# A wave-MLP kernel on one core: the first mix matmuls placed later in the order, the last outputs pipelined group by group, x added ahead in DRAM for the first two final steps

## The chip, the cores and the metric

The kernel runs on one core of one Trainium2 chip. The metric is the device time of one execution in microseconds (us). TensorE is PE in the profile, its weight loads PEld, VectorE is DVE, ScalarE is ACT, GpSimd is POOL, SyncE is SP. Times of kernels are medians of 4 to 5 runs (9 for the kernel before). A ratio is the mean time of one kernel's fast runs over that of the kernel before's fast runs of the same rounds, so it is not quite the ratio of the medians that stand beside it.

## The reference, cut to what matters

```python
# x: (8, 4224, 192).  First a causal convolution of 7 taps over the sequence, then:
theta = x @ w_theta
zr, zi = x * np.cos(theta), x * np.sin(theta)
y = einsum('ts,bsd->btd', w_tok_r, zr) + einsum('ts,bsd->btd', w_tok_i, zi)   # 4224 x 4224 each
u = x + y
return u + np.maximum(u @ w_ch, 0.0)
```

Nearly all arithmetic is in the two products with the 4224 x 4224 token matrices, called the *mix* below.

## The kernel before: the parts that matter

The sequence is cut into 33 *chunks* of 128 tokens. A chunk is prepared by: conv (PE) and its copy (ACT); two transposes (PE) and their copies to `uT` (ACT or DVE); two theta products (PE); sines (ACT); two products with x, `product(Z11)` and `product(Z21)`, and four subtractions, `sums` (DVE). They make seven operands, so that seven products do the work of eight.

A *step* is a pair of 128-row blocks of the output, mixed with up to 11 resident chunks (the one block left over makes a step of four runs). It has seven *runs*; each run is one matmul pair per chunk (a *slot*, 128x384 twice). At a run's end the PSUM tile is added into the SBUF tile `pv` by DVE, or copied by ACT: a *give*. There are two PSUM tiles `y`, so a run that opens a new tile waits until an earlier tile has been given. There are 58 steps in three groups of chunks; the last 17 are *final*: they add x, and then make the output (cast on ACT, transpose on PE, copy to `uT` on ACT, channel product on PE, ReLU and add on DVE, DMA out).

DVE also makes the weights of each step: it transposes tiles of the token matrices and forms sums and differences of them, called the *w differences* below.

In the profiles, L404 is the mix, L369 a give by DVE, L196 conv, L138 theta or the channel product, L238 a product with x, L244 the subtractions, L307 a weight transpose, L319 a w difference and L351 the addition of x on POOL. In the changed kernel the lines from L307 on stand one further (L405, L370, L308, L320, L352).

Each engine's order is fixed to the order in which the program emits its instructions. So the emission order in the start loop is an order of queues:

```python
    def between(n):                       # up to n slots of the mix, as far as chunks are ready
        left = more(n)
        if i < 2:
            idle(min(left, 1))            # filler matmuls on zeros
    for i in range(NW + 1):               # NW = 11 chunks; ch = chunk i, old = chunk i - 1
        if ch:  ch.conv(0)
        between(3)
        if old: old.theta(0)
        between(2)
        if ch:  ch.conv(1)
        between(3)
        if old: old.theta(1)
        # ... (loads of chunk i + 3)
        between(2)
        if ch:  ch.transpose(0)
        between(1)
        if ch:  ch.transpose(1)
        between(1)
        if old:
            old.product(Z11); old.product(Z21); old.sums(0); old.sums(1)
            ready[0] = i - 1              # from here the mix may use chunk i - 1
        between(2)
```

```python
    def add_x(self, i):                   # final steps
        if not self.late:                 # late: the last five steps
            xr = wk.tile([P, N], F16, name="xr", tag="xr", bufs=1)
            nc.sync.dma_start(out=xr, in_=xs[rows, :])
            pool(nc.gpsimd.tensor_tensor(out=self.pv[i], in0=self.pv[i], in1=xr, op=ALU.add))
            return
        for cols in (slice(0, HN), slice(HN, N)):      # accumulate in DRAM instead
            pool(nc.gpsimd.dma_start(out=part[...][self.tbs[i], :, cols],
                                     in_=xs[rows, cols], accum_op=ALU.add))
    # ... transposed(): uT = wk.tile([P, 6, P], F16, name="uT", tag="uT")   # two buffers
```

Of the kernel before, what the change touches and what calls it, by code (L numbers as in the profile page):

```python
# [16 lines left out]
def kernel(  # L17
# [42 lines left out]
    NU = (NT + 1) // 2  # L60
    NW = 11
# [5 lines left out]
    NSTEP = start[-1] + NU  # L67
# [13 lines left out]
    def pe(ins):  # L81
        return in_order("pe", ins)
# [7 lines left out]
    def pool(ins):  # L90
        return in_order("pool", ins)
# [68 lines left out]
    Z11, T1, Z21, Z22, T2, T4, T3 = range(7)  # L160

    class Chunk:


        def __init__(self, k, before=None):
            self.k = k
            self.xT = {}
            self.xw = wk.tile([2 * WR, 2, B, D], F16, name="xw", tag="big", bufs=6)
            for a in range(NQ):
                h, lo = a // 2, (a % 2) * WR  # L170
                t0 = token(k, a)
                hist = self.xw[lo : lo + HALO, h, :, :]
                if before is not None:
                    nc.sync.dma_start(
                        out=hist, in_=before.xw[lo + Q : lo + Q + HALO, h, :, :]
                    )
                elif t0 == 0:
                    nc.vector.memset(hist, 0.0)
                else:
                    lo, t0 = lo - HALO, t0 - HALO  # L180
                lo += HALO
                n = (a % 2 + 1) * WR - lo
                nc.gpsimd.dma_start(  # L183
                    out=self.xw[lo : lo + n, h, :, :],
                    in_=x[:, t0 : t0 + n, :].rearrange("b s d -> s b d"),
                )
# [74 lines left out]
    chunks = {}  # L261

    def load_chunk(k):
        if k < NK and k not in chunks:
            chunks[k] = Chunk(k, before=chunks[k - 1] if k % NW else None)

    def active(t):
        return [k for k in range(NK) if start[k] <= t < start[k] + NU]

    def unit(t):  # L270
        return (t + shift) % NU

    class Step:


        def __init__(self, t):
            self.t, self.u, self.ks = t, unit(t), active(t)
            self.n = len(self.ks)
            self.tbs = [tb for tb in (2 * self.u, 2 * self.u + 1) if tb < NT]
            self.pair = len(self.tbs) == 2  # L280
            self.first = t < NU
            self.final = t + NU >= NSTEP
            self.late = self.final and self.n < NW
            self.time = 0.324 * self.n * (7 if self.pair else 4)
            self.st, self.w, self.ub, self.uT, self.pv = {}, {}, {}, {}, []

# [58 lines left out]
        def add_x(self, i):  # L345

            rows = slice(self.tbs[i] * P, (self.tbs[i] + 1) * P)
            if not self.late:
                xr = wk.tile([P, N], F16, name="xr", tag="xr", bufs=1)
                nc.sync.dma_start(out=xr, in_=xs[rows, :])  # L350
                pool(nc.gpsimd.tensor_tensor(  # L351
                    out=self.pv[i], in0=self.pv[i], in1=xr, op=ALU.add  # L352
                ))
                return
            for cols in (slice(0, HN), slice(HN, N)):
                pool(nc.gpsimd.dma_start(
                    out=part[(self.t // NU - 1) % 2][self.tbs[i], :, cols],
                    in_=xs[rows, cols], accum_op=ALU.add,
                ))
# [83 lines left out]
        def outputs(self):  # L443

            found = []
            late = self.late and self.pair
            for i in range(len(self.tbs)):
                at = ((-self.time / 7 + 0.6, 1.2) if late else (0.7, 12.7))[i]
                cast, turn, mix = (1, 2.6, 4.4) if late else (2, 3.6, 5.4)
                for g in range(NG):  # L450
                    d = at + (3 if late else 3.6) * g
                    found.append((at + cast * g, lambda i=i, g=g: self.cast(i, g)))
                    found.append((d + turn, lambda i=i, g=g: self.turn_u(i, g)))
                    found.append((d + mix, lambda i=i, g=g: self.output(i, g)))
            return found

    steps = [Step(t) for t in range(NSTEP)]
# [5 lines left out]
    def step_events(t):  # L463
        found = []
        s = steps[t]
        if t + 1 < NSTEP:
            found += steps[t + 1].w_tasks()
            found.append((1.6, steps[t + 1].load_rows))
            if steps[t + 1].final and not steps[t + 1].late:
                for i in range(len(steps[t + 1].tbs)):  # L470
                    found.append((3.3 + 1.7 * i, lambda i=i: steps[t + 1].add_x(i)))
        if t + 4 < NSTEP and steps[t + 4].late:
            for i in range(len(steps[t + 4].tbs)):
                found.append((3.3 + 1.7 * i, lambda i=i: steps[t + 4].add_x(i)))
        if t + 2 < NSTEP:
            nxt = steps[t + 2]
            for m in (1, 2):
                found.append((1.3 + 3 * (m - 1), lambda m=m: nxt.load_w(m)))
        for at, f in outputs:
            begin = at - sum(s.time for s in steps[:t])  # L480
            if 0 <= begin < steps[t].time:
                found.append((7 * begin / steps[t].time, f))
        if t >= NU - 2:
            new = [k for k in range(NK) if start[k] == t + 2 and k >= NW]
            for k in new:
                found.append((4.5, lambda k=k: load_chunk(k)))
            at = 0.3
            for k in (k for k in range(NK) if start[k] == t + 1 and k >= NW):
                pos = [0, .5, 1.3, 1.6, 2.1, 2.5, 3.1, 3.15, 3.4, 3.6]

                def add(at, j, k):
                    def go():
                        if j == 0:
                            chunks[k].todo = chunks[k].tasks()
                        next(chunks[k].todo)()
                    found.append((at, go))
                for j, p in enumerate(pos):
                    add(at + p, j, k)
                at += 2.6
        return found  # L500


# [27 lines left out]
    def idle(n):  # L530
        for _ in range(n):
            pe(nc.tensor.matmul(
                spare[:, 0, 0:BH], lhsT=noise[:, 0:P], rhs=noise, start=True, stop=True
            ))
# [47 lines left out]
    def stream():  # L582
        for t in range(NSTEP):
            yield from steps[t].mix(step_events(t))

    ready = [-1]
# [3 lines left out]
    def more(n):  # L590

        for i in range(n):
            if need[0] is None:
                need[0] = next(flow, NK)
            if need[0] > ready[0]:
                return n - i
            need[0] = next(flow, NK)
        return 0
# [4 lines left out]
    load_chunk(2)  # L603
    for m in (1, 2):
        steps[1].load_w(m)
    for i in range(NW + 1):
        ch = chunks.get(i) if i < NW else None
        old = chunks[i - 1] if i else None

        def between(n):  # L610
            left = more(n)
            if i < 2:
                idle(min(left, 1))

        if ch:
            ch.conv(0)
        between(3)
        if old:
            old.theta(0)
        between(2)  # L620
        if ch:
            ch.conv(1)
        between(3)
        if old:
            old.theta(1)
        if i == 1:
            for _, f in steps[0].w_tasks():
                f()
        if i + 3 < NW:
            load_chunk(i + 3)  # L630
        between(2)
        if ch:
            ch.transpose(0)
        between(1)
        if ch:
            ch.transpose(1)
        between(1)
        if old:
            old.product(Z11)
            old.product(Z21)  # L640
            old.sums(0)
            old.sums(1)
            ready[0] = i - 1
        between(2)
    nc.vector.memset(wch[:, 1:3, :], 0.0)
    for rows, i, part_w in channel_pieces(moe_w_ch):
# [4 lines left out]
    for at, f in sorted(outputs, key=lambda e: e[0]):  # L651
        if at >= sum(s.time for s in steps):
            f()
# [28 lines left out]
```

## Time and profile before

| | before |
|---|---|
| time, median (3 runs at first, 1479.59 to 1481.64) | 1479.93 us |
| PE busy of the profiled span of 1478.3 us | 1435.8 us |
| PE idle 0 to 120 us | 20.7 us |
| PE idle 1020 to 1040 us | 7.0 us |
| PE idle 1440 us to the end | 12.6 us |

Two lines of the page of the kernel before: busy time by engine, and the engines' shares of the chain that ended last.

```profile
PE 1435.8 (97%) x10086; PEld 904.9 (61%) x10086; DVE 1030.6 (70%) x1050; ACT 361.8 (24%) x461; POOL 435.3 (29%) x655
...
PE 91%; DVE 3%; ACT 2%; DMA 1%; POOL 1%; issue 1%; SPq 0%; DVEq 0%; ACTq 0%; POOLq 0%
```

PE is the bound, so only its idle stretches can be won. The table by windows of the kernel before (window, length, busy us and count of PE, PEld, DVE, ACT, POOL, then granted clock, DMA share, GB/s) shows where they are; nearly all windows left out have PE at 20.00.

```profile
0.00:20.00 20.00, 13.89 (x118) 8.40 (x119) 8.21 (x26) 8.72 (x12) 17.50 (x40) 0.83 1.14 147
20.00:40.00 20.00, 13.29 (x99) 7.80 (x98) 14.46 (x24) 11.17 (x15) 9.73 (x18) 0.74 1.03 155
40.00:60.00 20.00, 16.57 (x150) 10.81 (x149) 15.03 (x24) 17.16 (x24) 11.20 (x20) 0.91 1.22 247
...
100.00:120.00 20.00, 18.72 (x135) 12.06 (x133) 19.15 (x23) 9.12 (x13) 4.29 (x8) 1.00 0.61 144
...
1020.00:1040.00 20.00, 13.04 (x82) 7.88 (x81) 19.57 (x20) 4.45 (x6) 5.40 (x5) 0.92 0.82 216
1440.00:1460.00 20.00, 17.90 (x147) 12.22 (x145) 14.64 (x17) 9.24 (x12) 0.00 (x0) 1.00 0.35 104
1460.00:1480.00 20.00, 7.82 (x74) 6.30 (x71) 5.65 (x6) 6.14 (x8) 0.00 (x0) 0.75 0.36 120
```

The timeline of the kernel before in the start (start us, length us, engine, line, operation, count, and in brackets the idle time before it and what ended it): the first mix matmuls of a chunk wait for its product, and the next chunk's conv (L196) stands behind them.

```profile
23.16 0.80 PE L404 MATMUL y<-z,wt 128*128 128x384 f16 x2 [1.35 <-DVE z L238]
...
24.21 0.85 PE L196 MATMUL pc<-xw,bands 96*64 96x192 f16 x8
...
32.96 1.44 PE L404 MATMUL y<-z,wt 128*128 128x384 f16 x4 [1.51 <-DVE z L238]
...
34.33 0.85 PE L196 MATMUL pc<-xw,bands 96*64 96x192 f16 x8
```

The timeline of the kernel before around 1020 us. Two POOL additions of x (L351) run while DVE has operations with two SBUF inputs (L319, L238), and DVE's pairs take 4.16 and 4.98 us instead of about 1.8. The give (L369) that PE waits for comes late.

```profile
1016.12 3.11 POOL L351 TENSOR_TENSOR pv<-pv,xr 128x1536 f32<-128x1536 f32 x1
1016.76 4.16 DVE L319 TENSOR_TENSOR wt<-wt 128x1408 f16<-128x1408 f16 x2
...
1028.26 4.98 DVE L238 TENSOR_TENSOR z<-z 128x1536 f16<-128x1536 f16 x2
1029.31 3.10 POOL L351 TENSOR_TENSOR pv<-pv,xr 128x1536 f32<-128x1536 f32 x1
1033.28 2.34 DVE L244 TENSOR_TENSOR z<-z 128x768 f16<-128x768 f16 x4
1035.54 0.95 DVE L369 TENSOR_TENSOR pv<-y,pv 128x768 f32<-128x768 f32 x1
...
1036.54 8.66 PE L404 MATMUL y<-z,wt 128*128 128x384 f16 x42 [5.20 <-DVE pv L369]
```

### The profile page before, as it was taken

What the parts mean: (1) busy time and instruction counts of PE and PEld (TensorE: products, weight loads), DVE (VectorE), ACT (ScalarE), POOL (GpSimd) and SP (SyncE); (2) the same over time, 40 slices, a digit from 0 to 9 for tenths busy, and PEclk for the clock granted to TensorE, in tenths of its full rate; (3) what the DMA queues carried; (4) which work ended last, traced back from release to release, by engine and by line L of the source; (5) the groups of instructions that cost most, each with busy time, mean ns of one, the idle gap of its engine ahead of it and who ended that gap; (6) DMA issues with size and microseconds to landing.
All of it is one profiled execution on the core that took longest, in us unless ns stands there. A gap on an engine that the chain in (4) does not pass through costs nothing.

```text
span 1478.3 us, 24435 instructions
## 1 busy us (share of the span) xinstructions
PE 1435.8 (97%) x10086; PEld 904.9 (61%) x10086; DVE 1030.6 (70%) x1050; ACT 361.8 (24%) x461; POOL 435.3 (29%) x655
## 2 busy tenths in 40 slices
PE   6899999999999999999999999998999999999996
PEld 3565666666666666666666666565566666666664
DVE  5894655454558787775766658778889888878675
ACT  4881101111134353000000015254112221212233
POOL 6431211111223322211111133233434343444220
PEclk7999999999999999999999999999999999999998
DMA  9986756564699999977778699999678787999873
GB/s 158 238 170 140 143 102 145 98 148 92 155 220 224 229 201 241 231 179 184 189 174 201 159 199 205 217 221 246 158 183 188 191 176 192 205 229 238 197 196 111
DMA packets 234400, 272.59 MB, mean 184 GB/s; under 512 B 69040, under 2 KB 202544, under 8 KB 234288
## 3 DMA queue, kind: packets, MB, share of 16 engines
q0 software_dynamic: 162464, 92.15, 47.9%
q1 hardware_dynamic: 71824, 178.88, 34.8%
q8 instruction: 79, 1.29, 0.4%
q14 instruction: 33, 0.27, 0.1%
HBM read 245.49 MB, written 108.13 MB: 239 GB/s over the span
## 4 chain that ended last, share of the span: by engine, by line
PE 91%; DVE 3%; ACT 2%; DMA 1%; POOL 1%; issue 1%; SPq 0%; DVEq 0%; ACTq 0%; POOLq 0%
PE y L404 82%; PE v L138 5%; PE tp L153 3%; PE pc L196 2%; DVE z L238 1%; ACT z L233 1%; DVE z L244 1%; POOL st L294 1%; DVE pv L369 1%; POOL xw L183 1%; DMA xw<-in_x_dram 1%; DMA part<-pv 0%; DVE wt L319 0%; DMA xw<-xw 0%; DVE wt L307 0%
## 5 line engine op out<-in xcount | busy, mean ns | idle before, releaser
L404 PE MATMUL y<-z,wt 128*128 128x384 f16 x7656 | 1299.7, 327 | 15.9 <-DVE pv L369 11.8
L404 PEld LDWEIGHTS <-wt 128*128 128x128 f16 x7656 | 738.7, 98 | 485.6 <-issue 23.0
L369 DVE TENSOR_TENSOR pv<-y,pv 128x768 f32<-128x768 f32 x324 | 308.4, 952 | 378.0 <-PE y L404 365.1
L307 DVE STREAM_TRANSPOSE wt<-st 128x1408 f16<-128x1408 f16 (+7 forms) x224 | 326.4, 1462 | 3.9 <-DMA st<-in_moe_w_tok_r_dram 2.1
L294 POOL DMA_DIRECT2D st<-in_moe_w_tok_r_dram x232 | 132.4, 579 | 490.8 <-DVE wt L307 473.4
L294 POOL DMA_DIRECT2D st<-in_moe_w_tok_i_dram x232 | 132.4, 579 | 473.9 <-DVE wt L307 460.4
L319 DVE TENSOR_TENSOR wt<-wt 128x1408 f16<-128x1408 f16 (+7 forms) x216 | 227.2, 1052 | 10.1 <-PE y L404 6.6
L148 ACT ACTIVATE uT<-tp 128x768 f16<-128x768 f16 x127 | 101.6, 811 | 304.6 <-PE tp L153 304.6
L148 ACT ACTIVATE z<-pc 128x768 f16<-128x768 f32 x65 | 52.8, 812 | 386.5 <-PE pc L196 386.5
L367 ACT ACTIVATE pv<-y 128x768 f32<-128x768 f32 x66 | 53.6, 812 | 278.1 <-PE y L404 271.7
L138 PEld LDWEIGHTS <-uT 128*128 128x128 f16 x1056 | 91.9, 99 | 25.3 <-ACT uT L148 5.3
L183 POOL DMA_DIRECT2D xw<-in_x_dram x132 | 76.2, 585 | 37.2 <-DVE wt L307 8.3
L433 DVE SCALAR_TENSOR_TENSOR pv<-v,pv 128x768 f32<-128x768 f32 x66 | 62.3, 948 | 26.9 <-PE v L138 24.1
L244 DVE TENSOR_TENSOR z<-z 128x768 f16<-128x768 f16 x132 | 73.6, 557 | 4.6
L423 ACT ACTIVATE ub<-pv 128x768 f16<-128x768 f32 x66 | 52.6, 836 | 94.5 <-DVE pv L369 76.6
L351 POOL TENSOR_TENSOR pv<-pv,xr 128x1536 f32<-128x1536 f32 x24 | 75.5, 3147 | 0.5 <-DMA xr<-xs 0.3
L233 ACT ACTIVATE z<-v,half_pi 128x768 f16<-128x768 f32 x66 | 59.5, 901 | 40.7 <-PE v L138 40.7
L238 DVE TENSOR_TENSOR z<-z 128x1536 f16<-128x1536 f16 x66 | 63.1, 997 | 3.1 <-ACT z L233 3.1
L138 PE MATMUL v<-wch,uT 128*128 128x192 f16 x528 | 55.2, 250 | 4.4 <-ACT uT L148 4.4
L138 PE MATMUL v<-wth,uT 128*128 128x192 f16 x528 | 55.0, 248 | 3.1 <-ACT z L233 3.1
L233 ACT ACTIVATE z<-v 128x768 f16<-128x768 f32 x66 | 53.1, 804 | 0.0
L153 PE MATMUL tp<-ident,z 128*128 128x128 f16 x396 | 33.8, 223 | 6.7 <-ACT z L233 6.3
(43 smaller groups left out, 193.3 us busy)
## 6 DMA issues: line engine op xcount, KB each, us to landing
part<-pv SPq DMA_DIRECT2D x79, 768.0 KB, 4.1
pv<-part SPq DMA_DIRECT2D x79, 768.0 KB, 5.3
out_dram<-pv SPq DMA_DIRECT2D x66, 384.0 KB, 4.5
st<-in_moe_w_tok_r_dram POOLq DMA_DIRECT2D x136, 176.0 KB, 5.7
st<-in_moe_w_tok_i_dram POOLq DMA_DIRECT2D x136, 176.0 KB, 4.7
xs<-z SPq DMA_DIRECT2D x132, 96.0 KB, 4.0
xw<-in_x_dram POOLq DMA_DIRECT2D x121, 96.0 KB, 6.3
xr<-xs SPq DMA_DIRECT2D x24, 384.0 KB, 3.6
```

Source lines behind the costliest of these rows:

```text
L138: pe(nc.tensor.matmul(v[:, k, b * D : (b + 1) * D], lhsT=tT[:, 3 * k + b + i, :], rhs=w[:, 2 * b + i, :], start=(i == 0), stop=(i == 1),))
L148: act(nc.scalar.activation(out=out, in_=in_, func=AT.Copy))
L153: pe(nc.tensor.transpose(tp[:, 0, k * P : (k + 1) * P], u[:, k * P : (k + 1) * P], ident))
L183: nc.gpsimd.dma_start(out=self.xw[lo : lo + n, h, :, :], in_=x[:, t0 : t0 + n, :].rearrange("b s d -> s b d"),)
L233: act(nc.scalar.activation(**args))
L238: dve(nc.vector.tensor_tensor(out=o, in0=xv, in1=o, op=ALU.mult))
L244: dve(nc.vector.tensor_tensor(out=z[:, o, :], in0=z[:, a, :], in1=z[:, b, :], op=ALU.subtract))
L294: pool(nc.gpsimd.dma_start(out=st[a * Q : (a + 1) * Q, 0:nb, :, 0:n] .rearrange("i r bt s -> i (r bt) s"), in_=w[self.tbs[0] * P : (self.t ...
L307: dve(nc.vector.transpose(self.w[name][:, 0 : self.n, :, :], self.st[int(name[1])][:, int(name[0]) - 1, :, 0 : self.n * Q] .rearrange("p b ...
L319: dve(nc.vector.tensor_tensor(out=self.w[name][:, 0 : self.n, :, :], in0=self.w[a][:, 0 : self.n, :, :], in1=self.w[b][:, 0 : self.n, :, : ...
L369: dve(nc.vector.tensor_tensor(out=o, in0=yv, in1=o, op=ALU.add))
L404: pe(nc.tensor.matmul(y[cn][:, q, 0:BH], lhsT=self.w[wn][:, c, :, :].rearrange("p bt i -> p (bt i)"), rhs=chunks[k].z[:, zn, q * BH : (q + ...
```

## The change

Its intent is to take PE's three idle stretches: in the start, mix matmuls no longer stand in front of the next chunk's preparation (the *deferral*); the two first final steps get x by accumulating DMAs ten steps ahead instead of POOL additions; the last outputs run group by group. The tasks of later chunks also move a little earlier in their steps.

```diff
+            self.ahead = self.late or 0 <= t + NU - NSTEP < 2
...
-            if not self.late:
+            if not self.ahead:                       # add_x: POOL addition only if not ahead
...
             for i in range(len(self.tbs)):           # outputs(); times in us from the step's end
-                at = ((-self.time / 7 + 0.6, 1.2) if late else (0.7, 12.7))[i]
-                cast, turn, mix = (1, 2.6, 4.4) if late else (2, 3.6, 5.4)
+                if self.late:
+                    at = 1.2 if i or not self.pair else 0.6 - self.time / 7
+                    every, turn, mix = 2.0, 1.2, 3.6
+                else:
+                    at = 0.7 + 12 * i
+                    every, turn, mix = 3.6, 2.9, 4.7
...
+        for s in steps[t:]:
+            if s.ahead and t == s.t - (4 if s.late else 10):
+                for i in range(len(s.tbs)):
+                    found.append((3.3 + 1.7 * i, lambda s=s, i=i: s.add_x(i)))
...
-            at = 0.3                                 # tasks of later chunks
+            at = 0.1
...
-                at += 2.6
+                at += 2.3
...
-    for i in range(NW + 1):                          # the start loop
+    for i in range(NW + 2):
...
-            if i < 2:
-                idle(min(left, 1))
+            if 0 < i < 3:
+                idle(min(left, 2))
...
             ch.conv(1)
+        if i == 0:
+            idle(4)
+        ready[0] = i - 2                             # the deferral
         between(3)
...
             ch.transpose(0)
+        if old:
+            old.product(Z11)                         # the earlier product
         between(1)
...
         if old:
-            old.product(Z11)
             old.product(Z21)
             old.sums(0)
             old.sums(1)
-            ready[0] = i - 1
         between(2)
```

More of the change, by code (lines that the diff above doesn't have):

```diff
@@ L445, in outputs @@
             found = []
-            late = self.late and self.pair
             for i in range(len(self.tbs)):
-                at = ((-self.time / 7 + 0.6, 1.2) if late else (0.7, 12.7))[i]
-                cast, turn, mix = (1, 2.6, 4.4) if late else (2, 3.6, 5.4)
+                if self.late:
[4 more added lines that the diff above has]
+                    every, turn, mix = 3.6, 2.9, 4.7
                 for g in range(NG):
-                    d = at + (3 if late else 3.6) * g
-                    found.append((at + cast * g, lambda i=i, g=g: self.cast(i, g)))
-                    found.append((d + turn, lambda i=i, g=g: self.turn_u(i, g)))
-                    found.append((d + mix, lambda i=i, g=g: self.output(i, g)))
+                    found.append((at, lambda i=i, g=g: self.cast(i, g)))
+                    found.append((at + turn, lambda i=i, g=g: self.turn_u(i, g)))
+                    found.append((at + mix, lambda i=i, g=g: self.output(i, g)))
+                    at += every
             return found
@@ L468, in step_events @@
             found.append((1.6, steps[t + 1].load_rows))
-            if steps[t + 1].final and not steps[t + 1].late:
+            if steps[t + 1].final and not steps[t + 1].ahead:
                 for i in range(len(steps[t + 1].tbs)):
                     found.append((3.3 + 1.7 * i, lambda i=i: steps[t + 1].add_x(i)))
-        if t + 4 < NSTEP and steps[t + 4].late:
-            for i in range(len(steps[t + 4].tbs)):
-                found.append((3.3 + 1.7 * i, lambda i=i: steps[t + 4].add_x(i)))
+        for s in steps[t:]:
+            if s.ahead and t == s.t - (4 if s.late else 10):
+                for i in range(len(s.tbs)):
+                    found.append((3.3 + 1.7 * i, lambda s=s, i=i: s.add_x(i)))
         if t + 2 < NSTEP:
@@ L605 @@
         steps[1].load_w(m)
-    for i in range(NW + 1):
+    for i in range(NW + 2):
         ch = chunks.get(i) if i < NW else None
-        old = chunks[i - 1] if i else None
+        old = chunks[i - 1] if 0 < i <= NW else None
         def between(n):
             left = more(n)
-            if i < 2:
-                idle(min(left, 1))
+            if 0 < i < 3:
+                idle(min(left, 2))
         if ch:
```

## The prediction

> **What bounds it now.** TensorE. The page gives PE 1435.8 of 1478.3 us busy (97%), and the chain that ended last is 91% PE. The table by 20 us windows shows 20.00 of 20 us in nearly all of them; the change removes no product, so only PE's idle stretches can be won. They lie in three places:
> - Start, 0 to 120 us: 20.7 us idle. A further 22 filler matmuls (noise, L532) and a granted clock of 0.67 to 0.83 between 10 and 40 us hide more.
> - 1020 to 1040 us: 7.0 us (PE waits for DVE pv L369, 1.75 and 5.2 us).
> - End: 2.1 us in 1440 to 1460, and about 10.5 us in 1460 to 1478.
>
> Two more stalls of 0.98 us (about 497 and 947 us) are the same kind as the second. Sum about 42 us.
>
> **The change, part by part.**
> 1. *Start.* At present a chunk's first mix matmuls stand in PE's order right behind its products, so PE waits (L404 <- DVE z L238: 1.35 and 1.51 us at about 23 and 33 us), and the next chunk's conv waits behind them; ACT idles 4.0 us at 25 us. Conv of chunks 1, 2, 3, 4 starts at 15.1, 24.2, 34.3, 44.4: about 10 us each, against some 6 to 7 us of serial ACT and PE work per chunk. Moved half an iteration later, the mix no longer holds conv: I expect chunk 3's conv near 28 us and the last (95.5 us now) near 85 to 87. From there on the period stays near 8.3 us, since DVE and ACT are over 90% busy (70 to 80 us window). Counting the loop, 7 of 117 chunk-slots of mixing (2 matmuls each, 2.3 us) shift behind the prep and must be subtracted. More fillers (28 after the first 8, from 14) fill PE waits; the Trainium skill (TensorE: Matmul & The Clock Gate, Part 1) says idleness halves the clock, which agrees with the 0.67 here. Gain 6.5 us (3 to 9).
> 2. *x ahead.* The two POOL adds of the first final step (3.1 us each, at 1016 and 1029) coincide with DVE's tensor_tensors: L319 x2 takes 4.16 us instead of 1.75, L238 x2 4.98 instead of 1.82, 5.6 us of DVE in a short step where DVE is 98% busy. The skill (SBUF, Who interferes with whom) has a two-input DVE operation contend with a GpSimd read; the trace agrees. These adds become eight accumulating DMAs ten steps earlier, where DMA is busy 0.67 to 0.79 and PE has no wait. Gain 6.5 us (5 to 7).
> 3. *Last outputs.* After the last mix (1458.4) PE, ACT and DVE alternate, each under 65% busy, until 1473.9, then 4.4 us of DMA. The new order interleaves turns and mixes of six pending groups. Following casts 0.84, transposes 0.5, evacuations 0.8, mixes 0.83 and DVE 0.96 us through two PSUM buffers, I estimate 10 us instead of 15.5. Gain 5.5 us (3 to 7).
> 4. *Chunk tasks* from 0.3/2.6 to 0.1/2.3: the late products move off the step's end; worth -1 to +2 us, counted 0.
>
> **Predicted:** 1479.9 - 18.5 = 1461.5 us; 80% range 1454 to 1469. Faster by over 2% (below 1450.3) 0.04, within 2% 0.955, slower 0.005.
>
> **What would show it.** PE idle in 0 to 120 us near 13; no wait of PE for pv L369 around 1020 to 1040, L319/L238 back to 0.9 us each; last DVE output about 10 us after the last mix; steady windows unchanged.
>
> **What would make it wrong.** Chunk loads landing too late to let conv run earlier (DMA share over 1.2 at 10 to 30 us); DVE saturated in the start so that PE waits reappear at 60 to 110 us; fillers delaying real work; products now colliding with the gives.

## The result, and the profile after

The changed kernel takes 1473.46 us (1472.75 to 1474.14, 4 runs) beside 1480.73 us for the kernel before in the same comparison: ratio 0.9951, interval 0.9934 to 0.9968. It is 7.3 us faster, where 18.5 us had been predicted, and the time lies above the predicted range of 1454 to 1469 us. The prediction was wrong; the steps of it that failed are named near the end.

The same two lines of the changed kernel's page. PE's share rises by one point only, and DVE's busy time falls by 30 us: 23 us of it are in the w differences (the group of L319, now L320, 227.2 to 204.0 us), which POOL no longer holds up as often. Most of that fall comes with the new order of outputs and is worth nothing: the group takes 225.8 us with x ahead alone (e3 below), and 210.0 us with the new outputs alone (e4), whose time did not change. It lies where PE does not wait for DVE.

```profile
PE 1435.7 (98%) x10100; PEld 905.6 (62%) x10100; DVE 1001.1 (68%) x1050; ACT 361.1 (25%) x461; POOL 429.4 (29%) x659
...
PE 87%; DMA 5%; DVE 4%; ACT 1%; issue 1%; SPq 0%; POOL 0%; DVEq 0%; ACTq 0%; POOLq 0%
```

The same windows of the changed kernel:

```profile
0.00:20.00 20.00, 14.36 (x114) 9.96 (x115) 8.09 (x26) 8.42 (x12) 17.45 (x40) 1.00 1.14 146
20.00:40.00 20.00, 15.14 (x149) 9.84 (x148) 17.29 (x28) 14.97 (x20) 11.95 (x21) 1.00 1.22 189
40.00:60.00 20.00, 14.95 (x124) 9.79 (x124) 12.77 (x20) 14.38 (x20) 8.87 (x16) 0.83 1.05 209
...
100.00:120.00 20.00, 16.71 (x103) 10.16 (x102) 19.46 (x23) 6.64 (x10) 4.86 (x9) 0.91 0.73 156
...
1020.00:1040.00 20.00, 19.20 (x139) 12.13 (x136) 18.38 (x22) 6.52 (x9) 4.38 (x8) 1.00 1.03 312
1440.00:1460.00 20.00, 16.88 (x146) 11.63 (x145) 13.88 (x16) 9.83 (x14) 0.00 (x0) 1.00 0.24 82
1460.00:1480.00 20.00, 4.68 (x54) 3.83 (x50) 4.69 (x5) 3.39 (x5) 0.00 (x0) 0.91 0.34 117
```

The stretch at 1020 us is repaired: 0.8 us idle instead of 7.0. The start is not. It is better from 20 to 40 us (idle 4.9 instead of 6.7 us) and worse from 40 to 60 (5.1 instead of 3.4) and from 100 to 120 (3.3 instead of 1.3); from 0 to 120 us PE is idle for 21.8 us, where I had predicted 13. At the end PE's idle time from 1440 us on falls from 12.6 to 10.7 us; the last DVE output comes 12.5 us after the last mix matmul in this trace and 14.3 us in a second trace of the same kernel (e17), where I had predicted 10.

The timeline of the changed kernel between 37 and 45 us shows the new wait. PE (L405) needs a give (L370, at 41.43). It stands on DVE behind the second product (L238), the four subtractions (L244) and a weight transpose (L308). Behind PE's blocked matmul stands theta (L138), and ACT waits 6.00 us for that.

```profile
37.11 0.55 PE L196 MATMUL pc<-xw,bands 96*64 96x192 f16 x8
37.56 0.95 DVE L238 TENSOR_TENSOR z<-z 128x1536 f16<-128x1536 f16 x1
...
38.55 2.34 DVE L244 TENSOR_TENSOR z<-z 128x768 f16<-128x768 f16 x4
40.80 0.70 DVE L308 STREAM_TRANSPOSE wt<-st 128x512 f16<-128x512 f16 x1
41.43 0.92 DVE L370 TENSOR_TENSOR pv<-y,pv 128x768 f32<-128x768 f32 x1
...
42.40 0.80 PE L405 MATMUL y<-z,wt 128*128 128x384 f16 x2 [3.89 <-DVE pv L370]
...
42.99 1.48 PE L138 MATMUL v<-wth,uT 128*128 128x192 f16 x8
...
44.52 0.90 ACT L233 ACTIVATE z<-v,half_pi 128x768 f16<-128x768 f32 x1 [6.00 <-PE v L138]
```

PE matmuls keep their program order (so says the Trainium skill, TensorE: Matmul & The Clock Gate, Part 2, step 1; the trace agrees, as theta at 42.99 us follows the blocked matmul at 42.40), so one blocked mix matmul blocks the preparation behind it. Two more such waits, 1.20 us at 86.85 and 3.29 us at 113.04, make 8.4 us in the start, against 1.9 us before. (Before, PE also waited 3.1 us for the products, L238; those waits are gone.)

The timeline of the changed kernel around 1020 us, for comparison: no POOL addition, the w differences at 0.89 us each, the products at their usual 1.82 us a pair, and 0.80 us of waiting instead of 5.20.

```profile
1018.48 0.89 DVE L320 TENSOR_TENSOR wt<-wt 128x1408 f16<-128x1408 f16 x1
...
1022.29 0.89 DVE L320 TENSOR_TENSOR wt<-wt 128x1408 f16<-128x1408 f16 x1
...
1028.60 1.82 DVE L238 TENSOR_TENSOR z<-z 128x1536 f16<-128x1536 f16 x2
1030.45 2.33 DVE L244 TENSOR_TENSOR z<-z 128x768 f16<-128x768 f16 x4
1032.70 0.95 DVE L370 TENSOR_TENSOR pv<-y,pv 128x768 f32<-128x768 f32 x1
...
1033.71 6.50 PE L405 MATMUL y<-z,wt 128*128 128x384 f16 x39 [0.80 <-DVE pv L370]
```

### The profile page after: what moved, and what is told of

Read it like the earlier page. It is cut to its first block, busy times and chain, and to the rows that moved or that the text cites. A ratio compares the mean times of both kernels' runs of the same rounds, so it can differ in the third digit from the quotient of the medians.

```text
span 1472.3 us, 24451 instructions
## 1 busy us (share of the span) xinstructions
PE 1435.7 (98%) x10100; PEld 905.6 (62%) x10100; DVE 1001.1 (68%) x1050; ACT 361.1 (25%) x461; POOL 429.4 (29%) x659
## 4 chain that ended last, share of the span: by engine, by line
PE 87%; DMA 5%; DVE 4%; ACT 1%; issue 1%; SPq 0%; POOL 0%; DVEq 0%; ACTq 0%; POOLq 0%
PE y L405 78%; PE v L138 5%; PE tp L153 2%; PE pc L196 2%; DVE pv L370 1%; DVE wt L308 1%; DMA part<-pv 1%; DMA xw<-xw 1%; DMA st<-in_moe_w_tok_i_dram 1%; DVE z L244 1%; DMA xw<-in_x_dram 1%; ACT z L233 1%; DVE z L238 1%; DMA pv<-part 1%; DVE pv L434 0%
## 5 line engine op out<-in xcount | busy, mean ns | idle before, releaser
L405 PE MATMUL y<-z,wt 128*128 128x384 f16 x7656 | 1297.6, 326 | 12.4 <-DVE pv L370 11.6
L405 PEld LDWEIGHTS <-wt 128*128 128x128 f16 x7656 | 738.4, 98 | 481.6 <-issue 17.5
L370 DVE TENSOR_TENSOR pv<-y,pv 128x768 f32<-128x768 f32 x324 | 308.6, 953 | 376.2 <-PE y L405 362.9
L308 DVE STREAM_TRANSPOSE wt<-st 128x1408 f16<-128x1408 f16 (+7 forms) x224 | 326.5, 1463 | 4.8 <-DMA st<-in_moe_w_tok_i_dram 4.6
L320 DVE TENSOR_TENSOR wt<-wt 128x1408 f16<-128x1408 f16 (+7 forms) x216 | 204.0, 945 | 10.9 <-PE y L405 8.2
L138 PEld LDWEIGHTS <-uT 128*128 128x128 f16 x1056 | 91.8, 98 | 24.0 <-issue 8.3
L244 DVE TENSOR_TENSOR z<-z 128x768 f16<-128x768 f16 x132 | 73.5, 557 | 4.2
L238 DVE TENSOR_TENSOR z<-z 128x1536 f16<-128x1536 f16 x66 | 60.6, 949 | 13.4 <-ACT z L233 13.4
L352 POOL TENSOR_TENSOR pv<-pv,xr 128x1536 f32<-128x1536 f32 x20 | 62.5, 3124 | 7.6 <-issue 6.9
L138 PE MATMUL v<-wch,uT 128*128 128x192 f16 x528 | 54.2, 246 | 3.9 <-DVE pv L434 2.2
L138 PE MATMUL v<-wth,uT 128*128 128x192 f16 x528 | 55.3, 248 | 1.4 <-ACT z L233 1.3
```

The source lines that it names most:

```text
L138: pe(nc.tensor.matmul(v[:, k, b * D : (b + 1) * D], lhsT=tT[:, 3 * k + b + i, :], rhs=w[:, 2 * b + i, :], start=(i == 0), stop=(i == 1),))
L238: dve(nc.vector.tensor_tensor(out=o, in0=xv, in1=o, op=ALU.mult))
L244: dve(nc.vector.tensor_tensor(out=z[:, o, :], in0=z[:, a, :], in1=z[:, b, :], op=ALU.subtract))
L308: dve(nc.vector.transpose(self.w[name][:, 0 : self.n, :, :], self.st[int(name[1])][:, int(name[0]) - 1, :, 0 : self.n * Q] .rearrange("p b ...
L320: dve(nc.vector.tensor_tensor(out=self.w[name][:, 0 : self.n, :, :], in0=self.w[a][:, 0 : self.n, :, :], in1=self.w[b][:, 0 : self.n, :, : ...
L370: dve(nc.vector.tensor_tensor(out=o, in0=yv, in1=o, op=ALU.add))
```

## The experiments

My theory after the result (A, later T1): adding x ahead gained all that was gained; the new start lost time, because gives stand on DVE behind products and subtractions; the outputs gained less than thought. The rivals: the start gained as predicted and something later took it back (B); the chunk tasks made the gain at 1020 us (C); the deferral or the fillers lose by themselves, whatever DVE does (T2).

A caution on the expectations. They count mix matmuls up to 200 us. Those counts took some matmuls twice, at window edges; in one window they are 785 before and 766 after. And e17 below, the changed kernel once more, has 786. So such a count from one trace scatters by 20 matmuls (3.2 us at 0.162 us each), and no conclusion below rests on it; they rest on the times, and on waits that repeat from trace to trace.

### Each part alone (e1 to e4, one chip)

**e1**, the changed kernel with the start loop of before.

```diff
 # the changed kernel, but the loop `for i in range(NW + ...)` as in the kernel before
```

> The changed kernel with the start loop of before. Counting mix matmuls in the two traces, the changed kernel is 23 of them (23 x 0.163 = 3.7 us) behind at 200 us. Theory A (the new start loses 3.7 us): about 1469.7 us, 0.9975 of the changed kernel. Rival B (the start gained as predicted and the loss lies later, in chunk tasks, extra DMA or the tail): 1477 us or more, slower than the changed kernel.

Measured: 1471.51 us (1468.00 to 1472.54), ratio 0.9934. The changed kernel has 0.9951: without the new start it would be 2.5 us (0.0017 x 1480) faster, which is within the uncertainty of the difference.

**e2**, the kernel before with the new start loop alone.

```diff
 # the kernel before, but the loop `for i in range(NW + ...)` as in the changed kernel
```

> The kernel before with the new start loop alone. Theory A: about 1484 us, 3.7 us slower than before, ratio 1.0025. Rival B (my prediction): about 1474 us, ratio 0.9956.

Measured: 1481.98 us beside 1480.81, ratio 1.0004 (0.9990 to 1.0018). The predicted gain of 6.5 us is excluded, and so is the low end of its range, 3 us. Both agree with a start that loses something, though less than the 3.7 us of the faulty count; that it loses is not shown by these two alone. Rival B falls.

**e3**, x added ahead alone.

```diff
 # the kernel before, with self.ahead, its two tests and the loop over steps[t:] of the change
```

> The kernel before with x added ahead for the first two final steps and nothing else. Theory A: the DVE holds go, 7.1 us faster (about 1473.5, ratio 0.9952), with PE's waits at 1020 to 1040 us falling from 7.0 to about 1 us. Rival C (the gain there came from the earlier chunk tasks, 0.1/2.3 in place of 0.3/2.6): under 4 us faster.

Measured: 1473.34 us, ratio 0.9948 (0.9935 to 0.9960), 7.7 us. The waits at 1020 us fall from 1.75 and 5.20 us to a single one of 1.62. This one part gives the whole gain of the change. The waits account for 5.3 us of it; the rest is within the scatter (in this trace the start was also 16 mix matmuls ahead at 200 us). Rival C falls.

**e4**, the new order of outputs alone.

```diff
 # the kernel before, with outputs() of the change
```

> The kernel before with the new order of outputs alone. Theory A: 3.4 us faster (about 1477.3, ratio 0.9977), the last DVE output 12.5 us after the last mix matmul, from 15.5. Rival: 5.5 us as predicted, the rest having been eaten by other parts.

Measured: 1480.67 us, ratio 0.9998 (0.9986 to 1.0011): nothing. Neither 3.4 nor 5.5 us came. In its trace the stretch from the last mix matmul to the last DVE output did shrink from 15.5 to 12.7 us, but the last mix matmul itself comes 1.5 us later (1459.9 instead of 1458.4): turns that stood behind it now stand in front of it. (Here the counts can be used: 7390 mix matmuls had been issued by 1400 us, 7389 before, but 7574 by 1440 us beside 7580.) The span ends 0.9 us sooner, which is below the scatter. My reading of the trace alone had counted the one end and not the other.

### Why the start gains nothing (e5 to e8, one chip)

**e5** and **e6** (on the changed kernel and on e1) take DVE work away, with a wrong result: three of four subtractions per chunk are left out in the start. All that is read is still written by something earlier.

```diff
 def sums(self, which):
-    for o, a, b in (((T3, Z22, T1), (T1, T1, Z11)), ((T2, Z22, T1), (T4, Z21, T2)))[which]:
+    pairs = (((T3, Z22, T1), (T1, T1, Z11)), ((T2, Z22, T1), (T4, Z21, T2)))[which]
+    if self.k < NW:
+        pairs = pairs[:1] if which == 0 else ()
+    for o, a, b in pairs:
```

> Wrong result on purpose: the changed kernel, but for the 11 chunks of the start three of the four DVE subtractions of each chunk are left out (33 x 0.57 = 19 us less DVE work before 115 us). Theory T1 (the new start gains nothing because DVE, with gives queued behind products and sums, holds PE): PE's waits for pv L370 before 130 us fall from 8.4 us to under 3 us and the time falls by about 6 us, to 1467.5. Theory T2 (fillers and deferred mixing themselves cost the gain): under 2 us faster.

> The same subtractions left out of the changed kernel with the old start (e1, 1471.5 us), as the control. T1: the old start is held by latency, not by DVE, so it gains less, about 2 us (1469.5), and the new start becomes the faster of the two by about 2 us. T2: the old start stays faster by 1 to 2 us.

Measured: 1464.75 us with the new start (ratio 0.9896) and 1467.83 with the old (0.9917). PE's waits for gives before 130 us fall from 8.4 to 3.1 us in e5. The new start gains 8.1 us from a lighter DVE (0.9951 - 0.9896 = 0.0055), the old one only 2.5 us, and the new start becomes the faster of the two by 3.1 us. So DVE is what keeps the new start from paying.

**e7** keeps the result and spreads the subtractions among later slots.

```diff
         if ch:
             ch.conv(0)
-        between(3)
+        between(1)
+        if 1 < i <= NW + 1:
+            chunks[i - 2].sums(1)
+        between(2)
...
             old.product(Z21)
-            old.sums(0)
-            old.sums(1)
-        between(2)
+        between(1)
+        if old:
+            old.sums(0)
+        between(1)
```

> The changed kernel, correct, with the two pairs of subtractions of each chunk spread between later mix slots, so that a give stands behind at most one pair. T1 as a matter of queue order: the 3.9 and 3.3 us waits for pv L370 fall below 2 us each, time 1469 to 1471. T1 as a matter of DVE's total work: waits move but do not shrink, time within 1 us of the changed kernel (1473.5).

Measured: 1472.03 us (ratio 0.9946), within the scatter of the changed kernel. The wait at 40 us splits into 2.58 and 0.79 us, and the one before 113 us (here before 109 us) stays at 3.28 us. At first sight that is the second form of T1: the waits move and hardly shrink. But the trace shows that the edit spread little. In 8 of the 11 chunks the four subtractions still run in one block, and only once does a give come between the two halves (at 39.59 us). At the late wait DVE's order is the old one:

```profile
106.09 2.34 DVE L244 TENSOR_TENSOR z<-z 128x768 f16<-128x768 f16 x4
108.34 0.95 DVE L370 TENSOR_TENSOR pv<-y,pv 128x768 f32<-128x768 f32 x1
...
109.34 20.85 PE L405 MATMUL y<-z,wt 128*128 128x384 f16 x117 [3.28 <-DVE pv L370]
```

So e7 does not decide between queue order and DVE's total work.

**e8** undoes the deferral alone.

```diff
-        ready[0] = i - 2
...
             old.sums(0)
             old.sums(1)
+            ready[0] = i - 1
         between(2)
```

> The changed kernel with its fillers and its earlier product, but the first mix matmuls of a chunk again placed right behind its sums. If the deferral is what loses time (T2), this is 2 us faster, at 1471.5. If the deferral gains but DVE takes it back (T1), this is no faster: 1473 to 1476, with waits of PE for DVE z L238 or L244 back at 1 to 2 us each.

Measured: 1468.14 us (1466.59 to 1470.42), ratio 0.9918. That is 4.9 us faster than the changed kernel (0.0033), and its direction was the forecast of T2 (which had said 2 us), not mine: T1 had said "no faster". The feared waits for the sums came to 1.43 us once. PE's waits for gives fall from 8.4 to 2.7 us. The DVE timeline of e8 in the same place as above shows why:

```profile
35.18 0.95 DVE L370 TENSOR_TENSOR pv<-y,pv 128x768 f32<-128x768 f32 x1
36.04 0.70 DVE L308 STREAM_TRANSPOSE wt<-st 128x512 f16<-128x512 f16 x1
36.67 0.92 DVE L370 TENSOR_TENSOR pv<-y,pv 128x768 f32<-128x768 f32 x1
37.51 0.41 DVE L320 TENSOR_TENSOR wt<-wt 128x512 f16<-128x512 f16 x1
37.84 0.95 DVE L370 TENSOR_TENSOR pv<-y,pv 128x768 f32<-128x768 f32 x1
38.70 0.94 DVE L238 TENSOR_TENSOR z<-z 128x1536 f16<-128x1536 f16 x1
```

Here three gives come before the products of chunk 2 (chunks are counted from 0). In the changed kernel the first comes at 36.69 us, and the other two, at 41.43 and 42.60, come behind that chunk's second product and its subtractions. The half iteration by which the mix is deferred puts its gives behind the next batch of preparation in DVE's queue. DVE's busy time is the same in both (1001.4 and 1001.1 us), so it is the order that differs. Conv of chunk 4 starts later than in the changed kernel (40.4 us instead of 37.1), but that of chunk 5 earlier (47.2 instead of 50.8), and the last at 90.5 instead of 92.6.

### Deferral, fillers, product, outputs (e9 to e12, one chip)

**e9**: e8 with the fillers of before; of the new start only the earlier product is left.

```diff
-            if 0 < i < 3:
-                idle(min(left, 2))
+            if i < 2:
+                idle(min(left, 1))
...
-        if i == 0:
-            idle(4)
```

> e8 (deferral undone, 1468.1 us) with the fillers of before as well; only the earlier first product stays of the new start. In e8's trace the mix is 27 matmuls (4.4 us) ahead of before at 200 us, with the clock at 1.00 in the first 130 us against 0.92. If the fillers give that: about 1471 to 1472, like e1 (1471.5), the clock in the first 40 us back to 0.7 to 0.8. If the earlier product gives it: within 1 us of 1468.1.

Measured: 1467.55 us (ratio 0.9915), the same as e8. Here the extra fillers are worth nothing that can be measured, and the clock in the first 40 us did not even fall back (1.00 in each window of 10 us of this trace). What is left of the new start is the earlier product: beside e1 it is worth 2.8 us (0.9934 - 0.9915).

**e10**: e8 with the subtractions left out (the edit of e5, a wrong result).

> Wrong result on purpose: e8 with the 33 subtractions left out as in e5 (1464.75). If the deferral loses because DVE is full, e8's lead of 5.3 us over the changed kernel shrinks here to under 2 us (1463 to 1466). If the deferral loses by itself (mixing moved behind the preparation), the lead stays near 5 us: about 1460.

Measured: 1465.06 us (ratio 0.9890), beside 0.9896 for e5. With a light DVE the deferral costs 0.9 us, which is inside the intervals; with the full DVE it costs 4.9. So both theories held one half: the deferral is what loses (T2 was right that undoing it pays), and it loses through DVE and not by itself (T1).

**e11**: e8 with one slot ahead of the subtractions.

```diff
             old.product(Z21)
+        between(1)
+        if old:
             old.sums(0)
             old.sums(1)
             ready[0] = i - 1
-        between(2)
+        between(1)
```

> e8 with one of the two last mix slots moved ahead of the four subtractions, so that less mixing waits directly behind them: a candidate. If the wait for z L244 (1.4 us) and the waits for pv L370 (2.7 us) are still worth something, 1466.5 to 1467.5; if not, within 1 us of 1468.1.

Measured: 1466.81 us (ratio 0.9908, interval 0.9894 to 0.9921, beside 0.9918 for e8): not distinguishable.

**e12**: e8 with the chunk tasks at 0.3 and 2.6 again.

```diff
-            at = 0.1
+            at = 0.3
...
-                at += 2.3
+                at += 2.6
```

> e8 with the chunk tasks of the later chunks at 0.3 and 2.6 again instead of 0.1 and 2.3. e1 (all but the start) was 1.8 us faster than e3 (x ahead alone) while the outputs alone gave 0.2: so if the chunk tasks are worth the rest, this is about 1.6 us slower, 1469.7, with new waits for pv L370 at about 490, 950 and 1030 us; if they are worth nothing, 1468.1.

Measured: 1467.89 us (ratio 0.9916): the moved chunk tasks are worth nothing that the times show, though two waits for gives near 493 and 943 us are 0.98 us with the old times and 0.73 with the new, and the one near 1026 us 1.62 with the old and 0.81 with the new.

### The outputs, and the product alone (e13 to e16, one chip)

**e13**: e8 with outputs() of before (the lines with - of that function in the change, put back).

> e8 (1468.1 us) with the order of outputs of before. If the new outputs are worth what e4 measured, within 1 us of 1468.1; if they are worth what the trace after the last mix shows, 3 us slower (1471); my prediction's 5.5 us would give 1473.6.

Measured: 1466.71 us (ratio 0.9904), if anything 2 us faster than e8. A second time the new order of outputs gains nothing.

**e14**: e8 with a third buffer for `uT` in the last five steps.

```diff
-        uT = wk.tile([P, 6, P], F16, name="uT", tag="uT")
+        if spare:        # every third transpose of the last five steps
+            uT = wk.tile([P, N], F16, name="xr", tag="xr", bufs=1)[:, 0 : 6 * P].rearrange(
+                "p (k s) -> p k s", s=P
+            )
+        else:
+            uT = wk.tile([P, 6, P], F16, name="uT", tag="uT")
```

> e8 with a third buffer for the transposed uT in the last five steps (an SBUF tile that is idle there). In e8 the evacuation to uT waits 0.97 and 0.59 us for the mix matmuls that read the older uT, the cast behind it on ACT is late, and PE waits 1.69 us for that cast. If that buffer is what the prediction's sum left out, the wait of 1.69 us goes and the last DVE output comes about 12.5 us after the last mix matmul instead of 13.7, time 1466.9. If PSUM or latency holds the tail anyway, no change (1468.1).

Measured: 1464.46 us (1462.59 to 1465.48), ratio 0.9888, correct. These are lines of e8's tail:

```profile
1449.45 0.81 ACT L148 ACTIVATE uT<-tp 128x768 f16<-128x768 f16 x1 [0.97 <-PE v L138]
...
1450.16 1.57 ACT L424 ACTIVATE ub<-pv 128x768 f16<-128x768 f32 x2
1451.05 0.51 PE L153 MATMUL tp<-ident,ub 128*128 128x128 f16 x6 [1.69 <-ACT ub L424]
```

ACT's copy into `uT` waits for the channel product (L138) that still reads the older buffer; the casts stand behind it on ACT; PE waits 1.69 us for a cast. The same place in e14:

```profile
1449.01 0.81 ACT L148 ACTIVATE uT<-tp 128x768 f16<-128x768 f16 x1
...
1449.70 1.58 ACT L431 ACTIVATE ub<-pv 128x768 f16<-128x768 f32 x2
...
1450.60 0.51 PE L153 MATMUL tp<-ident,ub 128*128 128x128 f16 x6 [0.61 <-ACT ub L431]
```

From the last mix matmul to the last DVE output e8 needs 13.5 us (1447.3 to 1460.8) and e14 10.7 us (1447.9 to 1458.7). The traced spans differ by 2.1 us, the times by 3.7 us (4.4 by the ratios); the intervals allow both. Without the extra fillers (e18 beside e9, below) the third buffer is worth 1.6 us, which is within the uncertainty; so the shorter tail is shown (10.7 us in the trace of e18 too), and its worth in the whole time is not settled.

**e15**: the kernel before with the earlier product alone.

```diff
             ch.transpose(0)
+        if old:
+            old.product(Z11)
         between(1)
...
         if old:
-            old.product(Z11)
             old.product(Z21)
```

> The kernel before with one line moved: the product for Z11 ahead of the second transpose's copy in DVE's order. e9 is 4.0 us faster than e1 by this line alone, so 1476.8 here (ratio 0.9973), the wait for z L238 before the first mix matmuls gone (3.1 us in the trace before) and conv of chunk 3 at about 29.5 us instead of 34.3. Rival: the line is worth it only with the other parts: 1480.8.

Measured: 1478.18 us beside 1480.34, ratio 0.9981 (0.9969 to 0.9994), 2.8 us. The waits for z L238 are gone (one of 1.60 us for the subtractions, L244, has come), and conv of chunk 3 starts at 29.8 us instead of 34.3. This one moved line takes away the waits at which the deferral was aimed.

**e16**: the changed kernel with the fillers of before (the edit of e9).

> The changed kernel (1473.5 us) with the fillers of before: deferral without the extra fillers. If fillers and deferral do not depend on each other, as e9 beside e8 suggests: within 1.5 us of 1473.5. If the fillers are what makes the deferral lose: about 1468.

Measured: 1475.53 us (1473.67 to 1477.61), ratio 0.9965. Its waits for gives in the start are those of the changed kernel (3.89, 1.20 and 3.28 us), so they do not come from the fillers. The 2 us to the changed kernel are at the edge of the scatter; whether fillers help a little where the mix is deferred stays open.

### Last checks (e17 and e18, one chip)

**e17** is the changed kernel without an edit, **e18** is e14 with the fillers of before (the edit of e9).

> The changed kernel, unchanged, on the chip of e18. If its first four runs stand for it: 1472.5 to 1474.5 us, ratio 0.994 to 0.996. If the difference of 2 us to e16 was scatter: up to 1475.5.

> e14 (1464.5 us: deferral undone, third uT buffer) with the fillers of before. If the extra fillers are worth nothing, as e9 beside e8 says: 1463.5 to 1465.5, some 9 us faster than e17. If they are worth the 2 us that e16 left: 1466.5.

Measured: the changed kernel again 1472.21 us, ratio 0.9951 as before, with the same three waits. e14 without the extra fillers: 1465.45 us (1462.83 to 1466.97), ratio 0.9904, not distinguishable from e14. So the best correct version (e14, 1464.5 us) is 1.1% faster than the kernel before and 0.6% faster than the changed kernel, with x ahead, the earlier product, the new outputs and a third `uT` buffer (and the extra fillers and moved chunk tasks, which nothing shows to matter). Of these, x ahead and the earlier product are shown to gain by themselves, and the new outputs are not. The third buffer was not tried with the old order of outputs.

## Why the prediction was wrong, point by point

| term | predicted gain | measured |
|---|---|---|
| start | 6.5 us (3 to 9) | none: a loss of 0.6 us alone (e2), of 2.5 us in place (e1) |
| x ahead | 6.5 us (5 to 7) | 7.7 us (e3) |
| last outputs | 5.5 us (3 to 7) | 0.3 us alone (e4), none in place (e13) |
| chunk tasks | 0 | none: a loss of 0.3 us (e12) |
| sum | 18.5 us | 7.3 us |

The measured column is ratio differences times 1480 us, each with an uncertainty of 2 us where it is a run beside the kernel before (e2, e3, e4), and of almost 3 us where it is a difference of two ratios.

- **The bound was right.** PE is the limit, and its three idle stretches are where the change acts.
- **x ahead was right in mechanism and size.** The Trainium skill (SBUF — State Buffer, Who interferes with whom) says that a DVE instruction with two SBUF inputs contends with a GpSimd instruction that reads SBUF. Before, DVE's pair of L319 took 4.16 us beside the addition; after, each takes 0.88 or 0.89 us.
- **The start was wrong in one step**: "Moved half an iteration later, the mix no longer holds conv: I expect chunk 3's conv near 28 us and the last (95.5 us now) near 85 to 87." The first half came true (29.1 us, chunk 4 at 37.1 instead of 44.4), the second did not (92.6 us). The step left out that the deferred mix brings its gives along, and that DVE's queue then has them behind a chunk's products and subtractions. The blocked PE holds theta, so ACT and then DVE run dry, and the lead of 7.3 us at chunk 4 has shrunk to 0.9 us at chunk 5 (50.8 instead of 51.7). "DVE saturated in the start so that PE waits reappear" stood in the list of what would make the prediction wrong, placed at 60 to 110 us and given no weight. e5, e6 and e10 show DVE as the cause, and e8 shows the deferral as the occasion: with DVE's full work the deferral costs 4.9 us, with the lighter work 0.9 us.
- **The start's gain was also put to the wrong part.** The wait that I had named (L404 for z L238) is taken away by the earlier product, which I did not cost at all: 2.8 us alone (e15). The deferral then takes away 4.9 us (e8), so that the start as a whole comes out some 2 us behind by these two numbers.
- **The fillers** were counted as filling waits and warming the clock. No worth is shown: without the extra fillers the time is 0.4 us shorter (e9 beside e8), 2.4 us longer (e18 beside e14) and 2.1 us longer (e16 beside the changed kernel), all within the uncertainty.
- **The outputs were mis-sized** in the term "through two PSUM buffers, I estimate 10 us instead of 15.5". The estimate left out the two `uT` buffers: e4 measured 12.7 us, and with a third buffer e14 measured 10.7. (Over all traces the stretch is 15.0 to 16.5 us with the old order, 12.5 to 15.1 with the new, and 10.7 in both traces with the third buffer.) It also left out that what is moved ahead of the last mix delays that mix (1.5 us in e4). In the whole time no gain of the new order is shown with two buffers (e4, e13).

## What to carry to other kernels

When work is deferred to free one engine, ask what the deferred work itself hands on, and behind what that will stand in the next engine's queue: here the matmuls were easy to delay, and their PSUM gives were not. Before moving a whole stage, look whether the wait it cures can be cured by moving the single producer: one product moved ahead by one line gave 2.8 us, where the large reordering gained nothing. A fall in an engine's busy time is worth nothing where nobody waits for that engine: the new outputs took 17.6 us from DVE (e4), and the time stayed. For a drain at the end, count every ring of buffers that the chain passes, SBUF as well as PSUM, and count what moving work forward does to the work that it passes.

## What the Trainium skill lacked or had wrong

- TensorE: Matmul & The Clock Gate, Part 1: the page gives activity as what restores the full clock. The trace agrees where PE fell idle (granted clock 0.66 between 40 and 50 us of the changed kernel, after the wait of 3.89 us). The page says nothing of filler matmuls in a kernel's start, and how little they can be worth: with 33 fillers (e8) or 22 (e9), the time is the same (1468.14 and 1467.55 us), and the first 40 us had the full clock in the trace of either. One trace does not settle this: with the fillers of e8, that of e10 shows a clock of 0.72 from 10 to 20 us.
- SBUF — State Buffer, Who interferes with whom: the contention is as the page says, but the page has it that whoever issues first gets the port. In the kernel before, a w difference that began at 1053.59 us, 0.67 us ahead of a POOL addition (1054.26 to 1057.36), still took 4.53 us instead of 0.88. It recurs: one that began at 1111.00 us, 0.51 us ahead of an addition, took 4.38 us. The profile's spans on POOL are rough, so this is a hint, and that the page is wrong is not shown.
- No page gives, in us of useful work, how much the start of one and the same program scatters from run to run: the changed kernel had issued 766 mix matmuls by 200 us in one trace and 786 in another (3.2 us), with the same waits for gives in both. Differences of that size need timed rounds, and not two traces.
